# Hashed attention and feed-forward on one core: the constant products at the start, the second pair's bits, and the order of the first pair's halves

## The chip, the cores and the metric

The kernel runs on one core of one Trainium2 chip. The metric is the device time of one execution in microseconds; the lower the better. Before the change it is 919.43 us, the median of 9 runs (918.22 to 920.29).

## What is computed

Two stages follow each other. The first is attention over 32 heads (4 batches of 8) of 768 tokens with 64 elements each, in which a query sees only the keys of its own hash bucket. The bucket is six bits, the signs of six projections:

```python
q_bits = (np.einsum('bhsd,dk->bhsk', q, proj) > 0).astype(np.int64)
k_bits = (np.einsum('bhsd,dk->bhsk', k, proj) > 0).astype(np.int64)
...
mask = q_bucket[:, :, :, None] == k_bucket[:, :, None, :]
scores = scale * np.matmul(q, k.transpose(0, 1, 3, 2))
scores = np.where(mask, scores, -1000000000.0)
...
attn = np.exp(scores)
attn = attn / (np.sum(attn, axis=-1, keepdims=True) + 1e-09)
return np.matmul(attn, v).astype(np.float32)
```

The second is a feed-forward layer on the 3072 rows of 512 that come out:

```python
h = x @ w_in
sp = np.maximum(h, 0.0) + np.log1p(np.exp(-np.abs(h)))
g = h * erf(sp)
return (g @ w_out).astype(np.float32)
```

## The kernel before

**Pairs, blocks, buffers.** The attention works on 16 pairs of heads; a pair's two heads stand in the two halves of the 128 partitions. The scores of a pair come transposed, keys on partitions and queries along the free dimension, in four groups `n` (half of the queries times half of the keys) of three blocks `c` (128 keys each). So group `n` of the whole stage belongs to pair `n // 4`, and block (n, c) is one PSUM buffer of two banks. There are three such buffers (`big`, `bufs=3`), handed out in turn: whoever takes one waits until the user three places earlier has been read. Score blocks and hash products take from the same three.

**Scores and the mask.** A block (`score`, L534) has two parts, which add up in PSUM: products of sign vectors in bf16 (`"b"`, from the tiles `both`), which give a huge negative number unless all bits agree, and the plain fp32 products of q and k. `plain` (L560) issues the fp32 part alone, before the signs exist. `exponential` (L568) is one ScalarE instruction over a block. `sum_keys` (L619) adds the exponentials up on VectorE, `weigh` (L631) multiplies them with v on TensorE, `leave_plain` (L696, tile `ev`) and `leave` (L690, tile `x`) take the result out.

**The bits of the first pair** are made in place, for half of the columns at a time. `hash_bits` (L373) multiplies q and k with the 64 columns of `proj_sb`, into PSUM partitions 0 to 63 for q and 64 to 127 for k. `sign_bits` (L386) takes the signs on ScalarE, `spread_bits` (L397, twice) scales the rows of k and `double_bits` (L407) copies those of q, both on VectorE. They fill `both[0]` at once, with no zeros needed beforehand.

**The bits of every later pair** go another way. `bits_of` (L812) multiplies with the 32 columns of `proj_q`: four products of q's and k's halves, each on 32 PSUM partitions. `sign_of` (L821) and `weigh_bits` (L831) make `sg`; `leave_bits` (L841) sends it to DRAM, and `place_bits` (L850) brings seven rows for each head back into `both[i % 2]`, whose other rows must be zero. So `both[1]` is cleared at the start (L433) and `both[0]`, which the first pair has filled, by `clean` (L859) once group 3 is done. All four DMAs and clearings are on GpSimd's queue, which also fetches the weights from piece 2 on (L456).

**Order.** What each engine runs in which order is fixed when the program is built. TensorE's order is written out by hand (the list `order`: group 0, groups 1 and 2, the bits of pair 1, `weigh` of groups 0 and 1, group 3, group 4, the bits of pair 2, and so on). `arrange` (L125) then simulates the engines with the costs given to `op` and `pe` and the delay `late` until a result reaches another engine; the place of every other instruction on ScalarE, VectorE, GpSimd and SP follows from that. Each engine runs its instructions strictly in that order, so one that waits holds up all behind it. The weights are converted between attention's instructions: two ScalarE steps (`square_high`, `keep_normal`, tile `keep`), then five on VectorE; in order, too.

**The start.** Before any data arrive, TensorE runs `WARM` products of constants. Each allocates the same PSUM bank anew and waits for the product before it. Then come the hash of the first pair's first half, that of its second half, and the two plain blocks (0, 0) and (0, 1).

Of the kernel before, what the change touches and what calls it, by code (L numbers as in the profile page):

```python
# [193 lines left out]
def kernel(  # L194
# [34 lines left out]
    small = ctx.enter_context(tc.tile_pool(name="small", bufs=3))  # L229
    QR = 32  # L230
    QB = QR // 2
    WARM = 5
    proj_sb = const.tile([P, 2 * QR], F32, name="proj_sb")
    weight = const.tile([P, 2], F32, name="weight")
    proj_q = const.tile([P, QR], F32, name="proj_q")
# [9 lines left out]
    blocks = []  # L245
    stats = const.tile([P, 2, NPAIR, 2], F32, name="stats")
    nc.vector.memset(ones, 1.0)
    nc.vector.memset(w_sum[:, 0, 0, 0:HS], 1.0)
    warm = w_sum[:, 0, 0, 0:HS]
    proj_in = const.tile([P, 2 * NBIT], F32, name="proj_in")  # L250
    nc.gpsimd.dma_start(out=proj_in, in_=proj2)
    nc.vector.memset(proj_sb, 0.0)
# [46 lines left out]
    def bank(name):  # L299
        return misc.tile([P, 512], F32, name=name, tag="bank")  # L300
# [45 lines left out]
    def fetch(i, load, quick=False):  # L346
        d = dict(
            q=load.tile([P, S], F32, name="q", tag="q"),
            k=load.tile([P, S], F32, name="k", tag="k"),
            v=load.tile([P, NC, P], F32, name="v", tag="v"),  # L350
        )
        b, j = divmod(i, JP)
        parts = ((0, "q"), (0, "k"), (1, "k"), (1, "q")) if quick else ((None, "q"), (None, "k"))
        for half, what in parts:
            cols = slice(0, S) if half is None else slice(half * HS, half * HS + HS)
            queue = nc.scalar if quick and what == "k" and half == 0 else nc.sync
            for ab in range(2):
                queue.dma_start(  # L358
                    out=d[what][ab * D : ab * D + D, cols],
                    in_=qkT[2 * i + ab, "qk".index(what) * D : "qk".index(what) * D + D, cols],  # L360
                )
        for ab in range(2):
            nc.sync.dma_start(  # L363
                out=d["v"][:, :, ab * D : ab * D + D],
                in_=v[b, 2 * j + ab].rearrange("(c p) d -> p c d", p=P),
            )
        return d
# [48 lines left out]
    def attention():  # L416
        NS = NPAIR * 4
        with (
# [11 lines left out]

            sg = bitp.tile([P, HS], BF16, name="sg")
            both = [bitp.tile([P, 2, S], BF16, name=f"both{n}") for n in range(2)]
            nc.gpsimd.memset(both[1], 0.0)  # L433
            junk = ep.tile([P, HS], BF16, name="junk")
            NE = 3 * GC
            e_all = ep.tile([P, NE, 2, HS + 1], F32, name="e_all")
# [339 lines left out]
                pairs[i] = fetch(i, load)  # L776

            pairs[0] = fetch(0, load, quick=True)
            for n in range(WARM):
                nc.tensor.matmul(  # L780
                    out=bank("warm")[:, 0 : 2 * P],
                    lhsT=warm[:, 0:P],
                    rhs=warm[:, P:HS],
                    start=True,
                    stop=True,
                )
            for half in range(2):
                hash_bits(pairs[0], big, (half,))
                take_bits(pairs[0], lambda what: both[0][:, "qk".index(what[0]), :], (half,))

            NH = NPAIR * 2
            ops = []

            def op(fn, args, engine, cost, rank, after=(), **more):
                name = (fn.__name__,) + args
                ops.append(Op(name, engine, cost, rank, lambda: fn(*args), after=after, **more))
# [7 lines left out]
            def bits_of(i):  # L804


                d = pairs[i]
                d["bits"] = big("bits")
                for n, what in enumerate("qk"):
                    for half in range(2):  # L810
                        row = (2 * n + half) * QR
                        nc.tensor.matmul(  # L812
                            out=d["bits"][row : row + QR, 0, 0:HS],
                            lhsT=proj_q,
                            rhs=d[what][:, half * HS : (half + 1) * HS],
                            start=True,
                            stop=True,
                        )
# [35 lines left out]
                        in_=bd[:, ab, 0 : NBIT + 1, :].rearrange("n r c -> r n c"),  # L854
                    )

            def clean():

                nc.gpsimd.memset(both[0], 0.0)  # L859

            chain = []
            order = [("score", 0)]
            for h in range(NH):
                order += [("score", n) for n in (2 * h + 1, 2 * h + 2) if n < NS]
                if h == 0:
                    order.insert(3, ("bits", 1))
                if h % 2 and (h + 3) // 2 < NPAIR:
                    order.append(("bits", (h + 3) // 2))
                if h >= 1:
                    order.append(("divisor", h - 1))  # L870
                order += [("weigh", 2 * h), ("weigh", 2 * h + 1)]
            slots = []
            for what, n in order:
                if what == "score":
                    i = n // 4
                    after = (("place_bits", i),)
                    if n == 0:
                        for c in range(2):
                            pe(plain, (n, c), 0.66)
                    for c in range(GC):  # L880
                        free = (slots[-3],) if len(slots) >= 3 else ()
                        pe(score, (n, c), 0.82 if n or c == 2 else 0.17, after + free)
                        slots.append(("exponential", n, c))
                elif what == "bits":
                    pe(bits_of, (n,), 0.92, (("start_pair", n), slots[-3]))
                    slots.append(("sign_of", n))
                elif what == "divisor":
                    pe(divisor, (n,), 0.42, (("sum_keys", n, last_sum(n)), ("keep_divisor", n - 1)))
                else:
                    h = n // 2  # L890
                    after = (("exponential", n, GC - 1),)
                    if n % 2 == 0:
                        after += (("leave", h - 1), ("leave_plain", (h - 1) // 2))
                    pe(weigh, (n,), 2.02, after)
# [42 lines left out]
            for i in range(NPAIR):  # L937
                n = 4 * i
                if i:
                    op(  # L940
                        start_pair,
                        (i,),
                        "SP",
                        3.6,
                        (0, n - 6),
                        (("weigh", n - 9), ("bits_of", i - 1))
                        + tuple(("measure", i - 3, m, half) for m in range(2) for half in range(2)),
                        late=3.5,
                    )
                    op(sign_of, (i,), "ACT", 0.6, (0, n - 6, 9), (("bits_of", i), ("leave_bits", i - 1)))  # L950
                    op(weigh_bits, (i,), "DVE", 0.33, (0, n - 6, 1), (("sign_of", i),))
                    op(leave_bits, (i,), "POOL", 0.7, (0, n - 6, 2), (("weigh_bits", i),), late=2.6)
                    op(
                        place_bits,
                        (i,),
                        "POOL",
                        1.2,
                        (0, n - 6, 3),
                        (("leave_bits", i), ("score", n - 5, 2)) + (("clean",),) * (i == 2),
                        late=2.6,  # L960
                    )
                for m in range(2):
                    for half in range(2):
                        op(
                            measure,
                            (i, m, half),
                            "ACT",
                            0.5,
                            (1, 2 * i + 2, 2 + m, half),
                            (("start_pair", i), ("score", n, 0)),  # L970
                        )
                if i == NPAIR - 1:
                    continue
                op(spread, (i,), "SP", 0.4, (0, n, 0), (("keep_divisor", 2 * i + 1),), late=3.0)
                op(gather, (i,), "SP", 0.35, (0, n, 1), (("spread", i),), late=4.5)
                op(invert, (i,), "DVE", 0.4, (0, n + 8, 3), (("gather", i),))
                op(ungather, (i,), "SP", 0.35, (0, n, 2), (("invert", i),), late=3.0)
                op(
                    widen,
                    (i,),  # L980
                    "SP",
                    1.1,
                    (0, n, 3),
                    (("ungather", i), ("normalise", i - 2)),
                    late=6.5,
                )
                op(normalise, (i,), "DVE", 0.95, (0, n + 8, 4), (("widen", i), ("leave", 2 * i + 1)))
                op(send, (i,), "SP", 0.35, (0, n, 4), (("normalise", i),), late=2.2)
            op(clean, (), "POOL", 1.4, (0, 0), (("score", 3, 2),), late=0.3)
            for n in range(len(pieces)):  # L990
                op(
                    fetch_weights,
# [771 lines left out]
```

## Time and profile before

| what | us |
|---|---|
| median of 9 runs | 919.43 |
| the profiled execution, in all | 920.04 |
| its span, first to last instruction | 918.2 |
| TensorE busy in the span | 904.4 |
| VectorE busy | 819.3 |
| ScalarE busy | 767.9 |
| GpSimd busy | 46.5 |

The span is what the trace covers; the execution's own time is 1.84 us longer. TensorE's matmuls are pipelined and their ends are modelled, so the start of the next one says more than the end of one. The first stage, attention, takes about the first third of the span; the times below are counted from the span's start. From 0 to 28 us TensorE is busy for 24.2 us and VectorE for 15.7; from 28 to 100 us TensorE is busy for 71.6 of 72 us, VectorE for 65.0 and ScalarE for 59.5.

A row of the timeline gives the start, the length, the engine, the line of the kernel, the operation with output and input, how many instructions were merged into the row and, in brackets, how long the engine had been idle and whose end released it.

### The profile page before, as it was taken

What the parts mean: (1) busy time and instruction counts of PE and PEld (TensorE: products, weight loads), DVE (VectorE), ACT (ScalarE), POOL (GpSimd) and SP (SyncE); (2) the same over time, 40 slices, a digit from 0 to 9 for tenths busy, and PEclk for the clock granted to TensorE, in tenths of its full rate; (3) what the DMA queues carried; (4) which work ended last, traced back from release to release, by engine and by line L of the source; (5) the groups of instructions that cost most, each with busy time, mean ns of one, the idle gap of its engine ahead of it and who ended that gap; (6) DMA issues with size and microseconds to landing.
All of it is one profiled execution on the core that took longest, in us unless ns stands there. A gap on an engine that the chain in (4) does not pass through costs nothing.

```text
span 918.2 us, 13120 instructions
## 1 busy us (share of the span) xinstructions
PE 904.4 (98%) x5006; PEld 659.2 (72%) x5006; DVE 819.3 (89%) x1020; ACT 767.9 (84%) x1002; POOL 46.5 (5%) x83
## 2 busy tenths in 40 slices
PE   9999999999999999999999999999999999999997
PEld 4444444444444478888888888888888888888885
DVE  4899999999899979899999799989899889988995
ACT  5788888788887739999998998899889997899892
POOL 1211111111111000000000000000000000000000
PEclk9999999999999999999999999999999999999999
DMA  8455567655574131102022111201220121011211
GB/s 205 110 159 163 142 179 204 186 149 164 152 193 138 59 122 64 46 1 104 12 70 80 36 46 69 81 35 46 70 81 35 35 75 40 36 35 46 69 35 49
DMA packets 62966, 83.05 MB, mean 90 GB/s; under 512 B 34174, under 2 KB 47342, under 8 KB 62896
## 3 DMA queue, kind: packets, MB, share of 16 engines
q1 hardware_dynamic: 56672, 64.08, 24.4%
q0 software_dynamic: 6064, 17.86, 6.3%
q8 instruction: 41, 0.67, 0.3%
q14 instruction: 29, 0.24, 0.1%
q10 hardware_dynamic: 160, 0.20, 0.1%
HBM read 64.71 MB, written 17.40 MB: 89 GB/s over the span
## 4 chain that ended last, share of the span: by engine, by line
PE 94%; DVE 2%; DMA 1%; SPq 1%; ACT 0%; issue 0%; POOL 0%; DVEq 0%; POOLq 0%
PE M L1323 31%; PE X L1183 28%; PE st L550 16%; PE av L631 14%; PE M L1183 3%; PE z_ps L666 1%; PE bits L812 1%; DMA q<-in_qkT_dram 1%; SPq L358 1%; DMA bd<-sg 0%; DVE e L1237 0%; DMA both<-bd 0%; DVE h L1265 0%; SPq L363 0%; DVE S L1280 0%
## 5 line engine op out<-in xcount | busy, mean ns | idle before, releaser
L1250 DVE SCALAR_TENSOR_TENSOR e<-w,e 128x1024 f32<-128x1024 f32 x144 | 173.3, 1219 | 5.8 <-ACT w L1246 3.0
L568 ACT ACTIVATE e_all<-st 128x768 f32<-128x768 f32 x192 | 151.2, 813 | 15.4 <-PE st L550 14.5
L1246 ACT ACTIVATE w<-w,cq 128x1024 f32<-128x1024 f32 x144 | 160.6, 1143 | 1.9
L550 PE MATMUL st<-q,k 64*128 64x384 f32 x768 | 155.3, 483 | 0.0
L1323 PE MATMUL M<-w_out_sb,h 128*128 128x256 f32 x576 | 140.2, 379 | 0.4 <-DVE h L1265 0.4
L631 PE MATMUL av<-e_all,v 128*64 128x385 f32 (+1 forms) x768 | 131.1, 490 | 0.0
L1183 PE MATMUL X<-x,w_in_sb 128*128 128x256 f32 x512 | 121.1, 379 | 0.0
L1323 PEld LDWEIGHTS M<-w_out_sb,h 128*128 128x128 f32 x576 | 109.3, 190 | 15.9 <-DVE h L1265 1.1
L1183 PEld LDWEIGHTS X<-x,w_in_sb 128*128 128x128 f32 x512 | 97.0, 190 | 13.8 <-ACT h L1201 0.6
L631 PEld LDWEIGHTS av<-e_all,v 128*64 128x64 f32 x768 | 52.3, 136 | 67.5 <-issue 66.3
L1323 PE MATMUL M<-wt,S 128*128 128x256 f32 x384 | 93.4, 379 | 0.4 <-DVE S L1280 0.4
L550 PEld LDWEIGHTS st<-q,k 64*128 64x128 f32 x768 | 68.5, 188 | 34.3 <-issue 33.6
L1183 PE MATMUL X<-x_sum,w_sum 128*128 128x256 f32 x344 | 81.7, 380 | 1.8 <-ACT h L1201 1.8
L1323 PEld LDWEIGHTS M<-wt,S 128*128 128x128 f32 x384 | 72.9, 190 | 10.7 <-DVE S L1280 0.8
L1183 PEld LDWEIGHTS X<-x_sum,w_sum 128*128 128x128 f32 x344 | 65.0, 190 | 12.0 <-ACT h L1201 3.3
L1201 ACT COPY h<-X 128x512 f32<-128x512 f32 x85 | 49.0, 576 | 22.3 <-PE X L1183 21.4
L1227 DVE SCALAR_TENSOR_TENSOR w<-w,e 128x1024 f32<-128x1024 f32 x48 | 58.4, 1220 | 9.7 <-ACT w L1222 9.6
L550 PE MATMUL st<-both 64*128 64x384 bf16 x384 | 63.4, 324 | 2.7 <-ACT keep L470 1.5
L1265 DVE TENSOR_TENSOR h<-h,e 128x1024 f32<-128x1024 f32 x48 | 57.9, 1220 | 5.8 <-ACT e L1261 5.5
L1241 ACT ACTIVATE w<-e 128x1024 f32<-128x1024 f32 x48 | 50.4, 1050 | 13.3 <-DVE e L1237 13.0
L1237 DVE TENSOR_TENSOR e<-e,w 128x1024 f32<-128x1024 f32 x48 | 57.4, 1217 | 2.7 <-ACT e L1233 2.6
L1205 DVE TENSOR_TENSOR h<-X,h 128x512 f32<-128x512 f32 x65 | 44.8, 689 | 16.4 <-PE X L1183 15.4
(133 smaller groups left out, 1376.1 us busy)
## 6 DMA issues: line engine op xcount, KB each, us to landing
wt<-wt SPq DMA_DIRECT2D x24, 768.0 KB, 4.1
raw<-in_w_out_dram POOLq DMA_DIRECT2D x16, 512.0 KB, 4.2
raw<-in_w_in_dram POOLq DMA_DIRECT2D x14, 512.0 KB, 4.3
v<-in_v_dram SPq DMA_DIRECT2D x32, 192.0 KB, 4.8
xs<-x SPq DMA_DIRECT2D x16, 384.0 KB, 2.4
q<-in_qkT_dram SPq DMA_DIRECT2D x30, 192.0 KB, 4.2
k<-in_qkT_dram SPq DMA_DIRECT2D x30, 192.0 KB, 4.4
r<-rd SPq DMA_DIRECT2D x30, 192.0 KB, 3.5
```

The source lines that it names most:

```text
L550: nc.tensor.matmul(out=st[:, ab, 0:HS], lhsT=d["k" + src][rows, keys], rhs=d["q" + src][rows, cols], start=(part == 0), stop=(part == 1),)
L568: nc.scalar.activation(out=e[:, :, 0:HS], in_=st[:, :, 0:HS], func=AF.Exp, scale=scale)
L631: nc.tensor.matmul(out=d["av"][rows, 0:w], lhsT=d["v"][:, g * GC + c, rows], rhs=e[:, ab, 0:w], start=(g == 0 and c == 0), stop=(g == 1 an ...
L1183: nc.tensor.matmul(out=d[where][:, u, :], lhsT=a[:, kc, f : f + P], rhs=b[:, kc, :], start=(first and u == 0 and kc == 0), stop=(last and ...
L1201: nc.scalar.copy(out=quarter(p, q), in_=st[p][where])
L1227: nc.vector.scalar_tensor_tensor(out=w, in0=w, scalar=-1.0, in1=st[p]["e", v], op0=ALU.add, op1=ALU.subtract)
L1237: nc.vector.tensor_tensor(out=s, in0=s, in1=st[p].pop(("w", v)), op=ALU.subtract)
L1241: nc.scalar.activation(out=z, in_=st[p]["s", v], func=AF.Square)
L1246: nc.scalar.activation(out=q, in_=z, func=AF.Square, bias=cq[:, j : j + 1])
L1250: nc.vector.scalar_tensor_tensor(out=s, in0=st[p].pop(("q", v, j)), scalar=ERF_Q[j][1], in1=s, op0=ALU.add, op1=ALU.mult,)
L1265: nc.vector.tensor_tensor(out=h, in0=h, in1=st[p].pop(("s", v)), op=ALU.mult)
L1323: nc.tensor.matmul(out=banks[name][:, sub, :], lhsT=a[:, u, sub * P : (sub + 1) * P], rhs=b[:, u, :], start=(c == 0 and k == 0), stop=(c = ...
```

## The change

Three things change together.

The constant products become ten of 64x128 in place of five of 128x256. Both operands are the tile `ones` (the moving one is its first column, repeated), all write the same allocation of one bank, and none waits for another. The clearing of a part of `w_sum` to ones, their former operand, goes.

Between the hash of the first pair's first half and that of its second half, the two plain blocks (0, 0) and (0, 1) are issued.

The second pair's bits are made in place like the first pair's, over all 768 columns at once: `bits_of(1)` is `hash_bits` with 64 columns and both halves, then come one sign instruction on ScalarE (`place_first`), two scalings (`weigh_first`) and one copy (`double_first`) on VectorE. Its DRAM round trip goes. Since `both[1]` is now filled with signs, it is cleared after group 7 instead of at the start, so `clean` exists for both tiles.

```diff
-    WARM = 5
+    WARM = 10
...
-    nc.vector.memset(w_sum[:, 0, 0, 0:HS], 1.0)
-    warm = w_sum[:, 0, 0, 0:HS]
...
-            nc.gpsimd.memset(both[1], 0.0)
...
+            warm = bank("warm")
             for n in range(WARM):
                 nc.tensor.matmul(
-                    out=bank("warm")[:, 0 : 2 * P],
-                    lhsT=warm[:, 0:P],
-                    rhs=warm[:, P:HS],
+                    out=warm[0:D, 0:P],
+                    lhsT=ones,
+                    rhs=ones[:, 0:1].broadcast_to([P, P]),
...
                 take_bits(pairs[0], lambda what: both[0][:, "qk".index(what[0]), :], (half,))
+                if half == 0:
+                    for c in range(2):
+                        plain(0, c)
...
             def bits_of(i):
+                if i == 1:
+                    hash_bits(pairs[i], big)
+                    return
...
-            def clean():
-
-                nc.gpsimd.memset(both[0], 0.0)
+            def place_first():
+
+                cols = slice(0, S)
+                sign_bits(pairs[1], lambda what: both[1][:, "qk".index(what[0]), :], cols)
+
+            def weigh_first(ab):
+                spread_bits(pairs[1], slice(0, S), ab)
+
+            def double_first():
+                double_bits(pairs[1], slice(0, S))
+
+            def clean(n):
+
+                nc.gpsimd.memset(both[n], 0.0)
...
+                    if i == 1:
+                        op(place_first, (), "ACT", 0.9, (0, n - 2, 9), (("bits_of", i),))
+                        for ab in (1, 0):
+                            op(weigh_first, (ab,), "DVE", 0.43, (0, n - 2, 1), (("place_first",),))
+                        op(double_first, (), "DVE", 0.35, (0, n - 2, 2), (("weigh_first", 0), ("weigh_first", 1)))
+                    else:
...
+            for n in range(2):
+                op(clean, (n,), "POOL", 1.4, (0, 4 * n), (("score", 4 * n + 3, 2),), late=0.3)
```

The planner's `late` of `leave_bits` and `place_bits` goes from 2.6 to 3.6, and `place_bits(i)` waits for `clean(i - 2)`, which concerns pairs 2 and 3 alone.

What the built program's lists show beyond the diff: apart from the instructions named here, the order on TensorE, ScalarE, VectorE and SP is as before. On ScalarE the second pair's sign was ahead of three of the first pair's squares (`measure`, L651) and now stands behind them. On VectorE the two scalings and the copy stand where the one scaling of `sg` stood, ahead of the conversion of piece 0 and of `ev`. On GpSimd `clean(0)` is now the first thing after the two small loads, ahead of weight piece 2, and `clean(1)` stands between piece 4 and the third pair's `leave_bits`.

More of the change, by code (lines that the diff above doesn't have):

```diff
@@ L865, in attention @@
                 if h == 0:
-                    order.insert(3, ("bits", 1))
+                    order.append(("bits", 1))
                 if h % 2 and (h + 3) // 2 < NPAIR:
@@ L875, in attention @@
                     i = n // 4
[L876 to L879, printed above, removed]
+                    after = (("double_first",) if i == 1 else ("place_bits", i),)
                     for c in range(GC):
@@ L884, in attention @@
                 elif what == "bits":
-                    pe(bits_of, (n,), 0.92, (("start_pair", n), slots[-3]))
-                    slots.append(("sign_of", n))
+                    pe(bits_of, (n,), 0.92 if n > 1 else 1.44, (("start_pair", n), slots[-3]))
+                    slots.append(("sign_of", n) if n > 1 else ("place_first",))
                 elif what == "divisor":
@@ L949, in attention @@
                     )
[L950 to L961, printed above, removed]
+                    if i == 1:
[4 more added lines that the diff above has]
+                    else:
+                        op(sign_of, (i,), "ACT", 0.6, (0, n - 6, 9), (("bits_of", i), ("leave_bits", i - 1)))
+                        op(weigh_bits, (i,), "DVE", 0.33, (0, n - 6, 1), (("sign_of", i),))
+                        op(leave_bits, (i,), "POOL", 0.7, (0, n - 6, 2), (("weigh_bits", i),), late=3.6)
+                        op(
+                            place_bits,
+                            (i,),
+                            "POOL",
+                            1.2,
+                            (0, n - 6, 3),
+                            (("leave_bits", i), ("score", n - 5, 2), ("clean", i - 2)),
+                            late=3.6,
+                        )
                 for m in range(2):
@@ L988, in attention @@
                 op(send, (i,), "SP", 0.35, (0, n, 4), (("normalise", i),), late=2.2)
-            op(clean, (), "POOL", 1.4, (0, 0), (("score", 3, 2),), late=0.3)
+            for n in range(2):
+                op(clean, (n,), "POOL", 1.4, (0, 4 * n), (("score", 4 * n + 3, 2),), late=0.3)
             for n in range(len(pieces)):
```

## The prediction

> **What bounds the kernel now.** First the page: busy rows and chain.
>
> ```profile
> PE 904.4 (98%) x5006; PEld 659.2 (72%) x5006; DVE 819.3 (89%) x1020; ACT 767.9 (84%) x1002; POOL 46.5 (5%) x83
> ...
> PE 94%; DVE 2%; DMA 1%; SPq 1%; ACT 0%; issue 0%; POOL 0%; DVEq 0%; POOLq 0%
> ```
>
> TensorE ends last and nearly never rests, so a microsecond won at the front reaches the end unless a later wait takes it. The waits of PE from 28 us to the end sum to only 3.7 us. Nearly all that the change touches lies before that, so next comes the timeline from 0 to 32 us, TensorE first (start, length, engine, line):
>
> ```profile
> 1.40 6.34 PE L780 MATMUL warm<-w_sum 128*128 128x256 f32 x10 [1.40 <-DVE w_sum L248]
> 7.67 0.90 PE L373 MATMUL bits<-q,proj_sb 128*64 128x384 f32 x1
> ...
> 8.36 0.84 PE L373 MATMUL bits<-q,proj_sb 128*64 128x384 f32 x1
> ...
> 9.00 0.53 PE L373 MATMUL bits<-q,proj_sb 128*64 128x384 f32 x1
> ...
> 9.36 0.49 PE L373 MATMUL bits<-q,proj_sb 128*64 128x384 f32 x1
> ...
> 17.39 0.52 PE L812 MATMUL bits<-q,proj_q 128*32 128x384 f32 x2
> ...
> 27.33 0.33 PE L550 MATMUL st<-both 64*128 64x384 bf16 x1 [0.74 <-DMA both<-bd]
> ...
> 28.08 0.39 PE L550 MATMUL st<-both 64*128 64x384 bf16 x2
> ```
>
> Two losses show. The constant products hold the first hash until 7.67, and its passes of 384 columns then come 0.69 and 0.64 apart, against 0.36 for the second half: the array ran at half rate until about 9. And pair 1's first score block, due at 24.63 (three blocks of 0.805 after 22.20), is held: the block after it starts at 28.08, so the stall is 28.08 - 0.805 - 24.63 = 2.64 us. GpSimd shows its cause:
>
> ```profile
> 19.82 0.54 POOL L841 DMA_DIRECT2D bd<-sg  x1 [15.97 <-DVE sg L831]
> ...
> 24.06 1.14 POOL L850 DMA_DIRECT2D both<-bd  x2 [3.69 <-DMA bd<-sg]
> ```
>
> Pair 1's bits go to DRAM (3.6 us to land) and back (2.7), and nothing covers that for the second pair. ScalarE sets the rhythm at the front:
>
> ```profile
> 9.29 1.23 ACT L386 ACTIVATE both<-bits,sgn 128x384 bf16<-128x384 f32 x2 [5.96 <-PE bits L373]
> 11.57 5.92 ACT L568 ACTIVATE e_all<-st 128x768 f32<-128x768 f32 x8 [1.06 <-PE st L550]
> ...
> 64.45 0.68 ACT L470 ACTIVATE keep<-raw 128x512 f32<-128x512 f32 x1 [3.85 <-DMA raw<-in_w_in_dram]
> ```
>
> The third line is the weak place further on: weight piece 5 arrives late, exponentials queue behind it, and PE already loses 0.45 us there (at 67.01).
>
> **What the skill says.** "TensorE: Matmul & The Clock Gate", Part 1: the array starts at half clock and goes to full after a busy window of some 3.4 us, whose phase isn't tied to the kernel. The hash passes agree on the factor (0.64-0.69 against 0.36); the release came only at about 9.0 here, 7.6 us after the first product. The products of before were not dense: each took 1.28 us, about 0.85 of it streaming if its 2 x 256 columns cost what the slow hash did (0.64/384 per column), since each waited for the one before. "TensorEngine Tiling (Array Packing)", Theoretical Speedup: 32 columns of weights allow four tiles at once, 64 two. The trace agrees: pair 1's four products at 32 columns take 0.78 (17.39 to 18.17), and the four at 64 columns take 0.78 for each half. "VectorE: DVE Perf Modes", perf-mode tier table: 16-bit scale and copy run at up to four results a cycle; used below for lengths not in the trace.
>
> **The change, step by step.**
>
> 1. *Constant products.* They now need only the memset of ones (ends 0.93; w_sum's ended 1.34), so they start at 0.99. Ten of 128 columns, two passes each: 20 x 128 x 1.67-1.8 ns = 4.3-4.6 us at half clock, without waits between them: end about 5.4. The data are there: q's and k's first half landed by 4.3 (issue 1.4 plus 2.9), and proj_sb's copies ended 4.39. So the first hash moves from 7.67 to 5.4. Dense from 0.99, a whole busy window ends between 4.4 and 7.8 by the skill's figure; I take 6.1.
>
> 2. *Order of halves.* Hash one: 0.66 at full rate, 0.35 of it done by 6.1, so it ends 6.4. Eight plain passes (1.29) to 7.7, the second hash (0.72) to 8.4; its data landed by about 7.2. Sign starts 0.29 later, as before, and lasts 0.6. The two blocks' signed parts fit under it. First exponential: 9.3 instead of 11.57, a gain of 2.2. But the PSUM ring of three is used in another order: both plain blocks now hold buffers before the second hash, so block (0,2) must wait for the first exponential to end, where before block (1,0) was the first that had to. After 9.3 + 0.81 + 0.06 = 10.2 seven blocks follow instead of six: pair 1's hash starts at 10.2 + 7 x 0.805 + 0.1 = 15.9 instead of 17.39. Gain 1.5; 0.8 is lost to the ring. Pair 1's first k copy landed at 11.4 (7.28 + 4.1), its second, issued 0.6 later, I put at 12 to 13: no wait.
>
> 3. *Pair 1's hash at 64 columns.* 2 x 0.72 instead of 0.78: costs 0.65. av starts 17.3 instead of 18.17, gain 0.85.
>
> 4. *Signing in place.* Removed: both DMAs and 2.64 us of stall. Added on the path to block (4,0): Sign over 128x768 (0.83 by the 768-long exponential at 0.81), but behind three squares of 0.65 on ScalarE, so about 18.8 to 19.7. Two scalings of 64x768: 0.325 each at 384; at two results a cycle of that page's 0.96 GHz the extra 384 cost 0.2, so an estimated 0.52 (0.43 at four results, 0.65 doubled). Copy 0.35 (0.25 at 384). Ready at about 21.1; block (4,0) is due at 23.8. About 2.6 us of cover; a later Sign beyond that stalls PE one for one. Gain so far 0.85 + 2.64 = 3.5.
>
> 5. *What is late next.* DVE's 1.4 us stands in front of two weight steps (1.15) and then ev, which ScalarE's copy x<-av waits for, with the exponentials behind it. av ends at 21.35, but ev comes only about 22.4, so exponential (3,0) starts near 23.05, only 0.2 earlier than before. Block (4,0) takes its buffer: 0.1 of wait. A square of weights is between, so exponential (4,0) ends about 26.7 where pair 2's hash wants its buffer at 26.25: 0.45 more. Net 2.9. I take off 0.2 for DVE, which lags PE until its first idle places (1.9 us at 29.5).
>
> 6. *At nothing.* The memset of w_sum; the memset of both[1] at 2.45, idle GpSimd; weight pieces 0 and 1 (landed 16.4, 18.9, first used about 19.7). clean(0) moves ahead of piece 2, which needs piece 0's conversion (about 25) anyway. clean(1), 1.4 us, now stands on GpSimd between piece 4 and pair 3's bd; GpSimd is idle from 44.8 to 52.77 and block (7,2), which it waits for, ends at 46.95: 4.4 us of cover. SP's list is unchanged.
>
> Sum: 2.2 - 0.8 + 0.1 of rounding - 0.65 + 2.64 - 0.55 - 0.2 = 2.7. The profiled execution (918.2 span, 920.04 in all) would take 917.3; the median of nine, 919.43, is 0.6 below it, so I forecast 916.7.
>
> **Rivals.**
>
> *A, the queues don't bite.* Steps 5's 0.75 is not lost and the clock rises early (+0.4), and the 0.45 at 67 may go: gain 3.5-4.3, 915.5. For: these waits rest on tenths. Against: DVE is 90% busy from 28 to 100 us.
>
> *B, the clock stays low.* If constants on half the columns don't count as busy, the window must hold hash and scores, which begin at 5.4: release 9 to 12. The same sum with 9.0 gives 1.4, with 12 gives 0.5: 918.4. For: five full-width products did not release it before 9. Against: they had gaps.
>
> *C, the gain is swallowed.* DVE and ScalarE keep their old times after the front, and PE waits for weights or exponentials until 1 us is left: 918.4. For: step 5. Against: DVE and ScalarE have idle places of 1.9 and 2.8 us by 45.
>
> *D, slower.* clean(1) blocks GpSimd's queue. Behind it are pair 3's bd (52.77), its placing (58.93), then piece 5 (60.06, landing 64.4), for which ScalarE waits ahead of exponentials that PE needs. If its wait ends only after the scores at 59.5, bd goes at 60.9, 8.2 late, PE stalls as long: 919.43 - 2.7 + 8.2 = 924.9. It decides from a start later than 54.1. For: that chain is taut. Against: its reader is done at 46.95.
>
> **How the numbers follow.** Main case (gain 2.0-3.3) 0.50, A 0.18, B 0.20, C 0.06, D 0.06. The range goes from A's 915.0 to B's 918.9. Faster by over 0.2% (1.84 us, what can be told from no change): the main case and A nearly whole, part of B: 0.74. Within: B and C: 0.20. Slower: D, 0.06.
>
> **What would show it.** Step 1: first hash near 5.4, passes turning from about 0.65 to 0.35 before 8. Step 2: first exponential near 9.3, pair 1's hash near 15.9. Step 4: no DMA of bd before 28, block (4,0) near 23.9. Step 5: exponential (3,0) at 23, after ev. Step 6: clean(1) near 44.5. Wrong if the first hash's passes stay at 0.65 through the plain blocks, if block (4,0) waits for the copy, or if ScalarE's wait for piece 5 grows.

## The result and the profile after

The changed kernel takes 916.22 us, the median of 9 runs (915.01 to 916.78). The kernel before, run beside it, took 919.54 us (29 runs, 918.15 to 920.65). The ratio is 0.9964, with a 95% interval from 0.9956 to 0.9972: 3.3 us faster. The forecast was a gain of 2.7 and a time of 916.7.

| us | before | after |
|---|---|---|
| the profiled execution, in all | 920.04 | 915.46 |
| its span | 918.2 | 913.7 |
| TensorE busy | 904.4 | 902.2 |
| VectorE busy | 819.3 | 819.4 |
| ScalarE busy | 767.9 | 767.8 |
| GpSimd busy | 46.5 | 45.1 |

The two spans differ by 4.5 us, more than the medians do: the profiled execution of before lies 0.5 us above its median, that of after 0.8 below. The profile is read for where time goes, the medians for how much. TensorE is busy 2.2 us less and idle 2.3 us less. The page of after says who still sets the end:

```profile
PE 902.2 (99%) x5016; PEld 660.5 (72%) x5016; DVE 819.4 (90%) x1021; ACT 767.8 (84%) x1002; POOL 45.1 (5%) x80
...
PE 95%; DVE 2%; ACT 2%; issue 0%; DVEq 0%
```

The DMA's 1% of the chain is gone. The timeline of TensorE in after, from the start to pair 1's first block (start, length, engine, line, what, count, idle time and its releaser):

```profile
0.99 4.10 PE L778 MATMUL warm<-ones 128*64 128x128 f32 x20 [0.99 <-DVE ones L247]
5.04 0.51 PE L371 MATMUL bits<-q,proj_sb 128*64 128x384 f32 x1
...
5.38 0.49 PE L371 MATMUL bits<-q,proj_sb 128*64 128x384 f32 x1
...
8.99 0.34 PE L547 MATMUL st<-both 64*128 64x384 bf16 x2 [0.27 <-ACT both L384]
...
14.75 0.54 PE L371 MATMUL bits<-q,proj_sb 128*64 128x384 f32 x1
...
16.09 4.05 PE L628 MATMUL av<-e_all,v 128*64 128x385 f32 x24
...
22.51 0.33 PE L547 MATMUL st<-both 64*128 64x384 bf16 x2
```

(A pass is one run of a product through the array; an fp32 product shows as two.) The constant products now run in one piece; the first hash starts at 5.04 instead of 7.67, and its passes come 0.34 us apart at once, the full rate. Inside the first row the passes of the constant products are 0.21 us apart until 4.46 and 0.14 to 0.11 from then on: there the array went over to full rate. Block (0,2), at 8.99, waits 0.27 us for a sign, not for an exponential. Pair 1's hash comes at 14.75 (before 17.39), and block (4,0), at 22.51, waits for nothing. ScalarE and VectorE behind it, in after, each from its own timeline:

```profile
8.84 6.02 ACT L565 ACTIVATE e_all<-st 128x768 f32<-128x768 f32 x8
...
17.77 0.88 ACT L384 ACTIVATE both<-bits,sgn 128x768 bf16<-128x768 f32 x1
...
21.21 0.48 ACT L687 COPY x<-av 128x384 f32<-128x384 f32 x1 [1.23 <-DVE ev L693]
21.59 2.23 ACT L565 ACTIVATE e_all<-st 128x768 f32<-128x768 f32 x3
```

```profile
18.68 0.85 DVE L395 TENSOR_SCALAR both<-both,weight 64x768 bf16<-64x768 bf16 x2 [2.29 <-ACT both L384]
19.57 0.35 DVE L405 COPY both<-both 64x768 bf16<-64x768 bf16 x1
...
21.03 0.15 DVE L693 TENSOR_SCALAR ev<-av 128x1 f32<-128x1 f32 x1
```

Pair 1's bits are ready at 19.57 + 0.35 = 19.92, which leaves 2.6 us of cover. GpSimd's timeline in after shows the clearing that rival D feared, and the waits of TensorE show what is left:

```profile
41.85 1.38 POOL L874 MEMSET both<- 128x1536 bf16 x1 [0.42 <-PE st L547]
48.38 0.55 POOL L845 DMA_DIRECT2D bd<-sg  x1 [5.14 <-DVE sg L835]
```

```profile
PE st L547 <- ACT e_all L565: 0.7, 1, 0.7
...
PE st L547 <- ACT both L384: 0.3, 1, 0.3
```

In the second fence the columns are total, number and longest wait in us. The two waits of pair 1's block, 1.5 and 0.7 us in before, are gone; the wait at piece 5 (62.64 us) is 0.68 instead of 0.45. ScalarE's own wait for that piece, 3.85 us in before, is 4.07:

```profile
60.07 0.68 ACT L467 ACTIVATE keep<-raw 128x512 f32<-128x512 f32 x1 [4.07 <-DMA raw<-in_w_in_dram]
```

### The profile page after: what moved, and what is told of

Read it like the earlier page. It is cut to its first block, busy times and chain, and to the rows that moved or that the text cites. A ratio compares the mean times of both kernels' runs of the same rounds, so it can differ in the third digit from the quotient of the medians.

```text
span 913.7 us, 13137 instructions
## 1 busy us (share of the span) xinstructions
PE 902.2 (99%) x5016; PEld 660.5 (72%) x5016; DVE 819.4 (90%) x1021; ACT 767.8 (84%) x1002; POOL 45.1 (5%) x80
## 3 DMA queue, kind: packets, MB, share of 16 engines
q1 hardware_dynamic: 56672, 64.08, 24.8%
## 4 chain that ended last, share of the span: by engine, by line
PE 95%; DVE 2%; ACT 2%; issue 0%; DVEq 0%
PE M L1342 31%; PE X L1202 28%; PE st L547 16%; PE av L628 14%; PE M L1202 3%; PE z_ps L663 1%; PE bits L816 1%; ACT e_all L565 1%; PE warm L778 0%; DVE e L1256 0%; DVE h L1284 0%; DVE S L1299 0%; DVE h L1224 0%; DVE x_sum L340 0%; PE bits L371 0%
```

## The experiments

Eight runs were made. Four take the change apart; then one fills a gap, one drops the constant products, one repeats the changed kernel, and one moves piece 5. The account to be tested is the prediction's sum: each part brings its own term, and the terms add. Against it stood that the parts depend on each other: that the DRAM trip doesn't come earlier when the hash does, that inputs and not the products hold the first hash, and that what is won at the front goes into other waits. "At 30 us" below is the first product into `z_ps` behind pair 2's hash, at 30.52 in before's profile; such a place, found in each kernel's trace, is called a mark. Before ran beside each group: its median was 919.11 for the first four experiments and 919.41 for the last four. The ratio is taken from all the runs of both kernels and differs from the quotient of the medians by up to 0.0011, about 1 us.

| kernel | median us (runs) | ratio to before, 95% | at 30 us, against before |
|---|---|---|---|
| after | 916.22 (9) | 0.9964 (0.9956 to 0.9972) | -4.69 |
| after, again | 916.36 (7) | 0.9963 (0.9948 to 0.9978) | -4.33 |
| only signing in place | 918.58 (22) | 0.9990 (0.9982 to 0.9997) | -1.97 |
| only short products | 923.58 (6) | 1.0038 (1.0024 to 1.0053) | +2.99 |
| short products, new order | 922.76 (7) | 1.0038 (1.0025 to 1.0052) | +2.81 |
| the same, gap filled | 920.16 (12) | 1.0006 (0.9997 to 1.0014) | +0.66 |
| short products, in place, old order | 916.75 (15) | 0.9972 (0.9963 to 0.9980) | -4.27 |
| after, no constant products | 917.99 (20) | 0.9977 (0.9967 to 0.9988) | -3.21 |
| after, piece 5 earlier | 915.60 (6) | 0.9951 (0.9938 to 0.9964) | -4.65 |

### Signing in place alone

Before, with the second pair signed in place, `clean(1)` and the planner's new `late`; the five old products and the old order stay.

```diff
+                if i == 1:
+                    hash_bits(pairs[i], big)
+                    return
...
-            nc.gpsimd.memset(both[1], 0.0)
```

> The kernel before with the second pair's bits signed in place alone; constant products and order of the halves as before. Theory 1 (the parts add up along TensorE): the front up to pair 1's hash stays (17.4 us), the hash costs 0.6 more, the stall of 2.6 us before block (4,0) goes, a few tenths come back as waits for exponentials: 1.6 to 2.0 us faster than before, block (4,1) near 26.2 us. Rival (VectorE's longer chain takes the stall's place): block (4,0) waits for the copy until 26 us or later, and the gain is under 1 us.

Measured: ratio 0.9990, 0.5 us faster in the median. That is less than the 1.6 to 2.0 expected, but not for the rival's reason. TensorE's timeline of this kernel, at pair 1's first two blocks:

```profile
25.36 0.33 PE L549 MATMUL st<-both 64*128 64x384 bf16 x2
...
26.17 0.33 PE L549 MATMUL st<-both 64*128 64x384 bf16 x2
```

Both run without a wait: the stall is gone here too, and the mark at 30 us is 1.97 us ahead, 2.7 us from 187 us on. The front is still cold; the hash passes are 0.69, 0.64 and 0.58 us apart and reach full rate near 9.5. The median keeps less than the marks: before's profile lies 0.9 us above its median in this comparison, and the last pair of output DMAs on SP took 2.14 us in this profile against 0.83. 2.7 - 0.9 - 1.3 would leave the 0.5; this is an account of two single profiles, and why they differ in these two ways is open.

### Short products alone

```diff
-    WARM = 5
+    WARM = 10
...
+            warm = bank("warm")
...
-                    out=bank("warm")[:, 0 : 2 * P],
-                    lhsT=warm[:, 0:P],
-                    rhs=warm[:, P:HS],
+                    out=warm[0:D, 0:P],
+                    lhsT=ones,
+                    rhs=ones[:, 0:1].broadcast_to([P, P]),
```

> The kernel before with the short constant products alone. Theory 1: the first hash starts near 5.0 us, the second half's hash waits for its data until about 7.3, the first exponential comes near 9.7 instead of 11.6 and the whole DRAM trip of pair 1's bits starts 1.9 us earlier, so block (4,1) comes 1 to 1.9 us earlier than 28.08 and the median falls by 1 to 1.9 us. Rival (the trip is bound by the transfers ahead of it in the DMA engines, which are full until about 20 us): bd lands at 23.4 us as before, block (4,1) stays near 28.1, the stall grows to 4 us and the median stays within 0.5 us of before.

Measured: slower, ratio 1.0038, which neither account foresaw, although pair 1's hash came at 15.32, 2.07 us earlier than in before. GpSimd's timeline of this kernel, then TensorE's:

```profile
17.76 0.54 POOL L840 DMA_DIRECT2D bd<-sg  x1 [13.91 <-DVE sg L830]
23.93 1.14 POOL L849 DMA_DIRECT2D both<-bd  x2 [5.63 <-DMA bd<-sg]
```

```profile
27.10 0.48 PE L548 MATMUL st<-both 64*128 64x384 bf16 x1 [4.37 <-DMA both<-bd]
28.11 0.50 PE L548 MATMUL st<-both 64*128 64x384 bf16 x1 [0.54 <-DMA both<-bd]
28.12 1.78 PE L548 MATMUL st<-q,k 64*128 64x384 f32 x4
...
29.88 1.62 PE L548 MATMUL st<-q,k 64*128 64x384 f32 x4
```

The bits left for DRAM at 17.76, 2.06 us earlier than in before (19.82), and were fetched back at 23.93, 0.13 us earlier than in before (24.06). The DMA views of 10 to 28 us show where the lead went; the last figure is the median time from issue to landing, first in before, then in this kernel:

```profile
bd<-sg POOLq DMA_DIRECT2D x1, 96.0 KB, 3.6
both<-bd POOLq DMA_DIRECT2D x2, 21.0 KB, 2.4
```

```profile
bd<-sg POOLq DMA_DIRECT2D x1, 96.0 KB, 5.5
both<-bd POOLq DMA_DIRECT2D x2, 21.0 KB, 3.3
```

Sent 2 us earlier, the bits need 1.9 us longer. In both kernels SP issues loads until about 15 us and then none before 22; in the two-microsecond windows from 12 to 20 us the DMA share is 0.96 to 1.23 in before and 1.04 to 1.23 here, and only from 22 us on is it 0.03 in both. So the send seems to land when that burst of loads has drained. The two runs below agree: with new order, and with the gap filled, the bits leave at 18.50 and 18.18 and are fetched back at 23.52 and 24.67, and the DMA share is 0.64 and 1.10 from 20 to 22 us, 0.15 and 0.50 from 22 to 24. No run with fewer loads tried it. The return is slower too: SP issues pair 2's q and k at 22.84 here and at 24.90 in before, so they travel beside the return (DMA share 0.86 from 24 to 26 us, 0.06 in before).

So TensorE stands idle from 22.7 to 27.1, and then something new happens: its blocks last twice as long. The stage table of this kernel (busy time by engine, then the clock, the DMA share and GB/s) has it:

```profile
24.00:28.00 4.00, 0.48 (x1) 0.10 (x1) 3.39 (x4) 0.16 (x1) 2.96 (x4) 0.72 0.95 225
28.00:30.00 2.00, 1.89 (x8) 1.36 (x10) 0.00 (x0) 0.07 (x1) 0.00 (x0) 0.50 0.63 227
30.00:32.00 2.00, 2.00 (x10) 1.41 (x9) 0.00 (x0) 1.21 (x2) 0.00 (x0) 0.50 0.00 0
```

The columns are TensorE, its weight loads, VectorE, ScalarE and GpSimd. The clock is 0.50 from 25.8 to 32.6. The Trainium skill, "TensorE: Matmul & The Clock Gate", Part 1, says that an idle window of some 3.4 us puts the array back to half clock and a busy one releases it; the trace agrees in kind, with a fall 3.0 us after TensorE went idle at 22.73. In before TensorE's gap at this place, from 24.8 to 27.3, was shorter and broken by one product, and the clock stayed at 1.00:

```profile
26.27 0.32 PE L550 MATMUL st<-both 64*128 64x384 bf16 x1 [1.47 <-ACT keep L470]
```

The profile puts this first wait down to ScalarE's `keep`, which ended at 26.22; the first fetch of `both` (sent at 24.06, the quicker of the two took 2.1 us) can have landed at the same moment. That the whole stall hangs on the round trip is shown by the kernel with signing in place alone, where it is gone.

### Short products and new order, without signing in place

This is the kernel above with the two plain blocks between the halves.

```diff
+                if half == 0:
+                    for c in range(2):
+                        plain(0, c)
```

> Short constant products and the new order of the halves, without signing in place. Theory 1: pair 1's hash at 14.8 us as in the changed kernel, its bits back from DRAM 8.7 us later plus whatever the full DMA engines add, so block (4,0) waits for both<-bd by 3 us or more and the gain is 1.5 to 2.5 us. Rival (DMA engines full until 20 us): bd lands near 23 us whatever its issue, gain under 0.5 us.

Measured: the same ratio, 1.0038, slower again where a gain was expected. The bits leave at 18.50 and are fetched back at 23.52, TensorE waits 4.67 us, and its blocks run at half rate from 27.75 to 32.66. The order of the halves does not help while the round trip stands.

### The gap filled

The kernel above, with seven products of constants in front of pair 1's score blocks, 64x384 each, which nothing reads: added work, to keep the array busy in the gap.

```diff
+            def fill():
+                dummy = bank("dummy")
+                for _ in range(7):
+                    nc.tensor.matmul(
+                        out=dummy[0:D, 0:HS],
+                        lhsT=ones,
+                        rhs=ones[:, 0:1].broadcast_to([P, HS]),
...
+                    if n == 4:
+                        pe(fill, (), 0.01)
```

> Short products and new order without signing in place, plus seven constant products of 64x384 on TensorE just before block (4,0), where it stood idle for 4.7 us waiting for pair 1's bits; they add work and change no result. Theory 2 (the idle array fell back to half rate and ran the next 5 us slowly): with the gap filled the passes after 28 us come 0.33 instead of 0.64 apart and the kernel is about 2.4 us faster than the same one without filling, close to before. Rival (the slow passes come from contention with transfers, not from idling): the passes stay at 0.64 and the time stays 3.5 us above before or rises.

Measured: 2.6 us less than without the filling in the medians, 2.9 by the ratios; 2.4 were expected. TensorE's timeline:

```profile
21.95 4.76 PE L866 MATMUL dummy<-ones 128*64 128x384 f32 x14
27.90 0.42 PE L548 MATMUL st<-both 64*128 64x384 bf16 x2 [1.20 <-DMA both<-bd]
28.07 0.90 PE L548 MATMUL st<-q,k 64*128 64x384 f32 x4
28.74 0.39 PE L548 MATMUL st<-both 64*128 64x384 bf16 x2
```

A block again takes about 0.8 us. From the first plain part to pair 2's hash it is 30.51 - 28.07 = 2.44 us here and 32.84 - 28.12 = 4.72 us with the short products alone: the fall of the clock cost 2.3 us. The transfers were still under way (DMA share 0.78 from 28 to 30 us), so they are not what slows the passes. What is left is the round trip itself, which ends no earlier than in before, and the kernel can't be told from before (interval 0.9997 to 1.0014).

### After with the old order of halves

```diff
-                if half == 0:
-                    for c in range(2):
-                        plain(0, c)
```

> The changed kernel with the order of the halves as before (both hashes, then the two plain blocks). Theory 1 (the order uses TensorE's wait for the second half's data): the second hash starts not before about 7.3 us, plain blocks follow, the first exponential comes near 9.7 instead of 8.84 and the kernel is 0.7 us slower than the changed one, so 2.6 us faster than before. Rival (the data are there anyway): first exponential within 0.2 us of 8.84 and no difference.

Measured: 0.5 us above after's median (0.7 were expected), with intervals that overlap. TensorE's timeline at the two halves' hashes:

```profile
5.22 0.51 PE L371 MATMUL bits<-q,proj_sb 128*64 128x384 f32 x1 [0.47 <-DMA q<-in_qkT_dram]
...
6.82 0.51 PE L371 MATMUL bits<-q,proj_sb 128*64 128x384 f32 x1 [0.64 <-DMA q<-in_qkT_dram]
```

The second half is hashed before its data are there; in after the plain blocks fill that wait. The first exponential starts at 9.49 against 8.84, pair 1's hash at 15.31 against 14.75. But the wait at piece 5 is 0.2 here instead of 0.7: ScalarE starts on the piece at 59.87, in after at 60.07. At 30 us this trace is 0.43 us behind after's, at 70 us 0.18 ahead, and it ends 0.2 us ahead: what the order wins at the front, the wait for piece 5 takes back in these two traces.

### No constant products

```diff
-    WARM = 10
+    WARM = 0
```

> The changed kernel with no constant products at all. Theory 1 (they bring the array to full rate while the data come): the first hash starts at about 5.2 us, when its data land, but runs at half rate (passes 0.64 apart), and so do the plain blocks, until some 9 us or later; first exponential near 10.8 instead of 8.84, 1.5 to 2.5 us slower than the changed kernel. Rival (the arrival of the data sets the front, the rate hardly matters behind the ScalarE rhythm): within 0.5 us of the changed kernel.

Measured: 1.6 us slower than the unaltered after beside it (916.36); the intervals of the two ratios just overlap, but the trace is behind as well, by 1.1 us at 30 us and 1.4 at 70. TensorE's timeline:

```profile
5.17 0.87 PE L371 MATMUL bits<-q,proj_sb 128*64 128x384 f32 x1 [5.17 <-DVE steps L272]
...
5.84 0.85 PE L371 MATMUL bits<-q,proj_sb 128*64 128x384 f32 x1
...
6.75 2.25 PE L547 MATMUL st<-q,k 64*128 64x384 f32 x8
8.93 0.54 PE L371 MATMUL bits<-q,proj_sb 128*64 128x384 f32 x1
```

In no trace does the first hash start before 4.89, so the ten products cost next to nothing; without them its passes are 0.67 us apart, and the eight plain passes take 2.25 instead of 1.56 us: full rate is reached at 8.2, after 3.0 us of dense work. In before, with five products that wait for each other, it was reached at 9.1, 7.7 us after the first. Those products held the hash up, and the clock rose later in the two traces with them (9.1 and 9.5) than in this one without any.

### After again, and piece 5 earlier

The first is the kernel after, unaltered, run beside the second. The second lets pair 3's placing stand behind the fetch of weight piece 5 on GpSimd; nothing else differs in the source.

```diff
-                            (("leave_bits", i), ("score", n - 5, 2), ("clean", i - 2)),
+                            (("leave_bits", i), ("score", n - 5, 2), ("clean", i - 2)) + (("fetch_weights", 5),) * (i == 3),
```

> The changed kernel once more, unaltered, on another chip, for the spread and for a second trace. If the moment at which the array goes to full rate varies from run to run, this trace shows it elsewhere than at 5 us, and the front marks move by half of the difference; the median stays 3 to 3.5 us below before.

> The changed kernel with weight piece 5 fetched before the third pair's bits are placed, one swap on GpSimd's queue. Theory 3 (piece 5 holds up ScalarE and with it TensorE): ScalarE's wait of 4.07 us falls below 3, the 0.68 us wait of TensorE at 62.6 us goes, 0.5 to 0.7 us faster than the changed kernel. Rival (the wait moves to the bits of pair 3 or the next piece): no gain.

Measured: 916.36 and 915.60. TensorE's and ScalarE's timelines in the second trace of after:

```profile
5.31 0.75 PE L371 MATMUL bits<-q,proj_sb 128*64 128x384 f32 x1
...
5.90 0.49 PE L371 MATMUL bits<-q,proj_sb 128*64 128x384 f32 x1
...
63.23 0.34 PE L547 MATMUL st<-both 64*128 64x384 bf16 x2 [0.91 <-ACT e_all L565]
```

```profile
60.66 0.69 ACT L467 ACTIVATE keep<-raw 128x512 f32<-128x512 f32 x1 [4.29 <-DMA raw<-in_w_in_dram]
```

The same program reaches full rate at 5.8 here, against 4.5 in the first trace; pair 1's hash starts at 15.13 instead of 14.75. And with piece 5 earlier, GpSimd and then ScalarE:

```profile
49.14 0.53 POOL L453 DMA_DIRECT2D raw<-in_w_in_dram  x1 [0.17 <-issue]
54.42 1.15 POOL L854 DMA_DIRECT2D both<-bd  x2 [4.75 <-DMA bd<-sg]
```

```profile
55.94 0.70 ACT L467 ACTIVATE keep<-raw 128x512 f32<-128x512 f32 x1
```

The fetch goes out in GpSimd's idle time behind `bd`, ScalarE finds the piece there, and TensorE's wait of 0.7 to 0.9 us is gone from its list of waits; the placing itself comes at 54.42, against 53.72 and 54.44 in after's two traces. Between the marks at 59 and 70 us this kernel gains 0.63 us on before, while after loses 0.22 and 0.46 there. From 187 us on the marks are 0.8 us ahead of after's first trace and 1.4 of its second. The median is 0.76 us lower; since the intervals overlap, the trace shows this gain more surely than the medians. It has the lowest median of all the kernels run.

## Why the prediction came out right

The forecast of 916.7 lies 0.5 us above the median, and its sum of 2.7 us stands against 4.5 in the two profiles and 3.3 in the medians. The direction and the mechanism of each large term held. That the number came so near is in part luck: the sum was made for the profiles and is 1.8 short there. Taken from the two profiles, term by term:

| term of the sum | forecast | in the profiles | from |
|---|---|---|---|
| first exponential (steps 1, 2) | +2.2 | +2.73 | 11.57 - 8.84 |
| PSUM ring and rounding (step 2) | -0.7 | -0.09 | 17.39 - 11.57 = 5.82; 14.75 - 8.84 = 5.91 |
| hash at 64 columns (step 3) | -0.65 | -0.56 | 0.78 - 1.34 |
| stall of pair 1's block (step 4) | +2.64 | +2.68 | block (4,1): 28.08 - 23.32 = 4.76, less 18.17 - 16.09 = 2.08 |
| late next (step 5) | -0.55 | -0.07 | 30.52 - 25.83 = 4.69, less 4.76 |
| lag of DVE | -0.2 | -0.2 | 4.5 at the end, less 4.69 |

**Step 1** was right in kind and late in both times. The first hash came at 5.04 for 5.4. The release can be dated: the trace's record of the granted clock has its first entry, at full clock, at 9.07 us in before, between passes 0.64 and 0.36 us apart, and in after at 4.50, where the passes of the constant products change from 0.21 to 0.11. For 6.1 forecast that is 4.50 in one trace and 5.83 in another of the same program. In the seven traces with the ten short products it lies between 3.80 and 5.83, so 6.1 was late in all of them, and two (3.80 and 4.00) lie ahead of even the 4.4 that the prediction took for the earliest. That it moves by 1.3 us between two runs of one program agrees with a window that isn't tied to the kernel. It is also most of what the first exponential won over the forecast: in the second trace that comes at 9.22, in the first at 8.84, for 9.3. Rival B falls: constants on half the columns do count as busy. With the old products the release came at 9.07 and 9.52, without any at 8.18.

**Step 2** has the one term that failed, "0.8 is lost to the ring". I took the three buffers as handed out by position, so that block (0,2) had to wait for the first exponential; the description of the kernel before says the same and is wrong in this. Block (0,2) takes the buffer of the second hash, which is free as soon as its sign is done: it starts at 8.99, just after the sign (8.36 + 0.58 = 8.94) and ahead of the exponential's end at about 9.65. The ring cost 0.1. How the buffers are given out is read from these times; the views don't number them.

**Step 3** was sized about right; its "0.78 for each half" at 64 columns, though, was read from the second half alone, as the first took 1.33 at half rate (7.67 to 9.00). **Step 4** had the right mechanism and the right cover: the sign began earlier than forecast only because pair 1's hash did; the scalings took 0.85 together against an estimate of 1.04, so each took the 0.43 that the prediction gave for four results a cycle, and 2.6 us of cover stood where 2.6 were expected. **Step 5** named the right place, but the size was off. `ev` is 0.95 us behind the end of `av`, as forecast (1.05), and yet block (4,0) lost nothing, and pair 2's hash started 0.23 us after its last block was due, against 0.11 at pair 1's, so it lost about 0.1. The chain was shorter than forecast by tenths at two places: exponential (3,0) began 1.5 us behind the end of `av` for 1.7, and exponential (4,0) ended 3.5 us after that for 3.65. The 0.2 that was taken off for VectorE turned up elsewhere, mostly at piece 5: ScalarE starts on that piece 4.38 us earlier than in before, TensorE's mark at 59 us comes 4.60 earlier. So one of the prediction's signs of being wrong did show, in small: ScalarE's wait for piece 5 grew, from 3.85 to 4.07 (4.29 in the second trace). From the issue of the fetch to ScalarE's start it was 4.4 us in before and 5.1 to 5.2 in after. **Step 6** held: `clean(1)` ran at 41.85, with 5.14 us of idle GpSimd behind it, so rival D never came near its point.

The sum was too small by the ring (0.6), the first exponential (0.5) and step 5 (0.5), each on the same side. In the profiles rival A, in which the waits of step 5 are not lost and the clock rises early, is the nearer account, and 4.5 lies above even its 3.5 to 4.3; the median of 916.22 lies between the forecast and A's 915.5. Of the 4.5, a part is the luck of the two profiled executions (the second trace of after is 3.9 ahead of before from 187 us on); 3.3 is what nine and 29 runs give.

What the sum did not see is that its terms don't add freely. At 30 us, short products alone are 2.99 us behind before and signing in place alone is 1.97 ahead. Added, that is 1.0 behind; together, in the old order, they are 4.27 ahead. The 2.64 us of step 4 was taken as the stall of before, but with an earlier hash the round trip would have stalled TensorE for 5 us and put it to half rate, as it did with the short products alone. Signing in place is what lets the short products pay.

Two things stay open. How much of the 0.5 us between the old and the new order is real can't be told from these runs. And it was not tried whether a round trip started behind fewer loads would have come back earlier.

## What to carry to other kernels

Before you count a gain at the front, follow each transfer behind it: here one that was sent 2 us earlier into a burst of loads was fetched back only 0.1 us earlier, and the faster front only lengthened the gap. A gap of TensorE can cost twice, once as idle time and once as half rate afterwards: 4.4 us without work cost 2.3 more here, while a gap of 2.5 us with one product in it did not. Constant products in such a gap won that second cost back. Where buffers rotate, look in the trace at which reader releases the next user instead of counting places.

## What was not expected of the hardware

- Without anything between them, passes of 128 columns on half of the array's columns brought the full rate 2.8 to 4.8 us after the first of them (seven traces; in two of these the hash had begun). Passes of 256 columns on all of them, with gaps, had not done so when the hash came, and full rate followed 7.7 and 8.1 us after the first (two traces).
- At the start the clock column of the stage tables doesn't show the half rate: it reads 1.00 from 0 to 8 us in before, while the passes are 0.64 to 0.69 us apart. In the middle, with the short products alone, it does (0.50). The record behind the column has no entry before the release, and time without an entry counts as full clock. Where the first entry begins (9.07 us in before), the spacing of the passes changes too.
- The last pair of output DMAs on SP takes 0.83 us in four of the profiles (before and after among them) and 1.84 to 2.23 in the other six. The timelines of SP of after, in the first and then in the second trace of the same program:

```profile
907.76 0.83 SPq L1381 DMA_DIRECT2D out_dram<-u  x2
```

```profile
908.36 1.84 SPq L1381 DMA_DIRECT2D out_dram<-u  x2
```

Its cause is open. It adds 1.0 to 1.4 us to a span, so spans of single profiles can't be compared closer than that here; marks ahead of it can.
